# Scaling the rows of x before they are written, on 2048-byte rows, with the routing of the third batch moved forward

## The chip, the cores and the metric

The kernel runs on one core of a Trainium2 chip. The metric is the device time of one execution in microseconds (us). Three runs of the kernel before took 993.59, 993.12 and 991.86 us, median 993.12 us.

## The reference

Three layers follow each other. First an attention over 4 batches, 8 heads, 576 positions and 64 dimensions, causal, with a bias from a running sum of a positive part; its output is rearranged to x, 2304 rows (tokens) of 512. Then a mixture of 8 experts that picks one expert per row:

```
logits = x @ w_gate + modality_bias[modality_id]      # 2304 x 8
e_idx  = argmax(logits);  gate_w = softmax(logits)[e_idx]
h = relu(x[mask_e] @ w1[e])                           # 512 -> 1024
out[mask_e] = gate_w[mask_e] * (h @ w2[e])            # 1024 -> 512
```

Last a gated layer: `(sigmoid(x @ w_gate) * (x @ w_val)) @ w_out`, 512 to 1536 to 512. All data is 32-bit floating point. As the gate weight is positive, multiplying a row of x by it before w1 gives the same result as multiplying the output row.

## The kernel before

**Attention (the first 280 us).** The 32 heads are worked on in 16 pairs; a batch is four pairs. The order of all operations is written out by hand: `START` (L42) for the first pairs, then `PERIOD` (L27) once per pair. TensorE (PE) transposes and multiplies, VectorE (DVE) evacuates and subtracts, ScalarE (ACT) takes exponentials, GpSimd (POOL) prepares bias tiles (L170) and splits k and v (L194, L198). `norm` (L400) writes a pair's 128 columns of x into an SBUF tile `xr` of 128 x 5 x 513 elements; one batch is 576 rows, five row tiles.

**Router (class at L507).** When a batch is complete (`on_batch`, in `Ns` of its last pair) `batch` (L606) appends its work to one list `q`: logits, argmax and one-hot (L624 to L630, L653), the rank of each row in its expert (`ranks`, matmuls L637 and L639 and an addition L634), the exponential, then L658 to L665 on DVE. L662 makes `ix`, the place of each row in a table `tab` in DRAM; L665 writes the reciprocal of the sum, which is the gate weight, into column 512 of `xr`. Then for each of the five row tiles POOL scatters the row numbers into `tab` (L669, 128 elements of 4 bytes) and SP writes 128 rows of `xr` to x in DRAM (L673). The list is drained in two ways. During attention `tick` (L719) is called after certain operations of `PERIOD` (29 calls a pair) and takes one entry; `space(n)` entries are empty ticks and `GAP` adds empty ticks behind each entry. After attention `pump` (L726) takes up to 14 entries at a time and drops the empty ones. The rank matmuls of batches 0 to 2 ride along with the operation `txs` of a later pair, and the list is held until then; those of batch 3 run when the entry is reached.

**A guess (end of `batch`, b == 1).** After batch 1 the expert with most rows so far is taken; its first 512 rows are fetched (`fetch_rows` L701, an indirect DMA on POOL that waits for all scatters into `tab`), its weights are loaded by SP (`on_guess`), and slots 0 and 1 of 256 rows each work on them.

**Expert slots (class Moe, L866).** A slot gathers 2 x 128 rows by indirect DMA (L933), multiplies them by the gate weight in place (`gate` L940, on POOL; for slot 2 on DVE and ACT), transposes them on PE (`transpose` L948), and runs eight steps u. `step` (L1138) issues the first matmuls `mm1` (12) of step u and the second matmuls `mm2` (12) of step u - 1. Weights are loaded by `load_slot` and split into high and low halves by `split` (L913): ACT and DVE for w1, ACT and POOL (L909) for w2. `first` (L1125), called near the end of attention, gathers slots 0 and 1 and splits three steps on POOL alone. Step 0 runs inside the tail of attention.

**The hand-over (`early` L1159).** For u = 0 to 15 it issues step u, then `main(u)` (L1613), which pumps; when the list is empty it appends the table arithmetic of `slots` (L732, 58 entries, among them `fetch_rows` of all 40 slot rows, `indices`, which transposes them on PE (L711), and the copy to `rg`). Once the list is empty again `ready` is set, all engines read the flag `more`, and loads of slot 2 and gathers of slots 2 and 3 may start; then the next splits are issued (`aheads`). Each engine runs its instructions in the order in which they are issued here.

**Gated layer (class Moe2).** From 550 us to the end, after slots 2 to 8 and two half slots; nothing in it is touched.

Of the kernel before, what the change touches and what calls it, by code (L numbers as in the profile page):

```python
# [14 lines left out]
AF = mybir.ActivationFunctionType  # L15
ALU = mybir.AluOpType
# [4 lines left out]
TS = [64, 128, 128, 128, 128]  # L21
T0 = [0, 64, 192, 320, 448]
POS = [4, 0, 1, 2, 3]
RW = 513
CAP = 2304
BP, BT, WARM = 3, 3, 16
PERIOD = [  # L27
# [471 lines left out]
SPE = mybir.EngineType.SP  # L499
BIG = 100000.0  # L500
TROWS, PUMP = 96, 14
GAP, SP = [1, 1, 0, 0], [6, 3, 6, 0]
EARLY, EARLYB, MAIN, SLOTS, FIRST = 2, 2, 9, 14, 3
MAINH, HALVES, HROW, NROW = 2, 8, 32, 40


class Router:  # L507
# [98 lines left out]
    def batch(self, b, xr, lg):  # L606

        nc, cp, T = self.nc, self.cp, self.T
        V = nc.vector
# [8 lines left out]
        ex, se = tile_([128, 5, 8], "ex"), tile_([128, 5], "se")  # L618
        R, rk = tile_([128, 6, 8], "R"), tile_([128, 5], "rk")
        ix = tile_([128, 5], f"ix{b % 2}", U32)  # L620
        c, c1 = tile_([128, 8], "gc"), tile_([128, 8], "gc1")
        iob = self.iota.unsqueeze(1).to_broadcast([128, 5, 8])
        q = self.q
# [38 lines left out]
        q.append(lambda: V.tensor_scalar(ix, rk, 8.0 * CAP, None, ALU.add))  # L662
        q.append(lambda: V.tensor_reduce(se.unsqueeze(2), ex, axis=AX.X, op=ALU.add))
        q.append(lambda: V.tensor_scalar(se, se, 1e-9, None, ALU.add))
        q.append(lambda: V.reciprocal(xr[:, :, 512], se))  # L665
        for t in range(5):
            rows, r0 = (64, 0) if t == 4 else (128, 64 + 128 * t)
            self.space(SP[b])
            q.append(lambda t=t, rows=rows: self.apart("tab", nc.gpsimd.indirect_dma_start(  # L669
                out=self.tab.rearrange("r c -> (r c)").unsqueeze(1),  # L670
                out_offset=bass.IndirectOffsetOnAxis(ap=ix[:rows, t : t + 1], axis=0),
                in_=self.ids[:rows, b, t : t + 1], in_offset=None, bounds_check=TROWS * 256 - 1, oob_is_err=True)))
            q.append(lambda t=t, rows=rows, r0=r0: nc.sync.dma_start(  # L673
                self.x[b * self.S + r0 : b * self.S + r0 + rows, :], xr[:rows, t, :]))
# [49 lines left out]
                self.q[:0] = [None] * self.gap  # L724

    def pump(self, n):  # L726
        self.q = [f for f in self.q if f]
        while self.q and n:
            self.q.pop(0)()
            n -= 1  # L730

    def slots(self):  # L732

# [4 lines left out]
        nc, T, q = self.nc, self.T, self.q  # L738
        V = nc.vector
        n = self.cnt[self.B % 2]  # L740
# [6 lines left out]
        es, ep, s0, el, ch, g1, ex, z, base, void = (n1(nm) for nm in ("es", "ep", "s0", "el", "ch", "g1", "sx", "sz", "base", "void"))  # L747
        row, rg, tt = n1("row", U32), T([128, 3], "rg", I32), T([64, 1], "tt", I32)
        more = T([1, 1], "more", I32)
        bp = lambda a, w=9: a.to_broadcast([128, w])  # L750
        op = lambda f, *a, **kw: q.append(lambda: f(*a, **kw))
# [34 lines left out]

        expert(es)
        op(V.scalar_tensor_tensor, out=row, in0=ex, scalar=float(CAP // 256), in1=s0, op0=ALU.mult, op1=ALU.add)
        q.append(lambda: self.fetch_rows(self.tid, row, NROW))
        op(V.tensor_reduce, base, C, axis=AX.X, op=ALU.add)  # L790
        op(V.tensor_scalar, void, es, 9.0, float(CAP), ALU.is_equal, ALU.mult)
        op(V.tensor_tensor, base, base, void, ALU.add)
# [15 lines left out]
        op(V.tensor_reduce, s0[0:1], W[0:1, 1], axis=AX.X, op=ALU.add)  # L808
        op(V.tensor_scalar, s0[0:1], s0[0:1], float(MAINH), None, ALU.is_gt)
        op(V.scalar_tensor_tensor, out=more, in0=inc[0:1, 8:9], scalar=float(MAIN), in1=s0[0:1], op0=ALU.is_gt, op1=ALU.max)  # L810
        q.append(lambda: self.indices("idx", self.tid, NROW, self.B * self.S - 1))
        op(V.tensor_copy, rg[:, 2:3], base)
        self.rg, self.tt, self.more = rg, tt, more


# [50 lines left out]
class Moe:  # L866
    def __init__(self, tc, raw, ps, acc, router, w1, w2, x, x2, ids2, ident):
        self.tc, self.nc = tc, tc.nc
        self.acc, self.x2, self.ids2 = acc, x2, ids2
        self.raw, self.ps, self.r, self.w1, self.w2, self.x, self.ident = raw, ps, router, w1, w2, x, ident  # L870
        self.xg, self.xT, self.y, self.piece, self.regs = {}, {}, {}, {}, {}
        self.prev, self.hprev, self.pend, self.ready = None, None, [], False
        self.wbufs = 24

    def open(self, ctx, early):
# [49 lines left out]
    def rows(self, s):  # L925
        n = 576 * EARLYB if s < EARLY else 2304
        return self.x[:n, :], n - 1

    def gather(self, s):
# [6 lines left out]
                bounds_check=last, oob_is_err=True,  # L936
            )
        self.xg[s] = t

    def gate(self, s, quick=False):  # L940
        for c in range(1 if s >= HROW else 2):
            x = self.xg[s][:, c, :]
            if quick and c:
                self.nc.scalar.activation(x[:, :512], x[:, :512], AF.Copy, scale=x[:, 512:513])
                continue
            (self.nc.vector if quick else self.nc.gpsimd).tensor_scalar(x[:, :512], x[:, :512], x[:, 512:513], 1.0, ALU.mult, ALU.mult)

    def transpose(self, s, half):  # L948
        nc = self.nc
# [77 lines left out]
    def simple_slot(self, s):  # L1027
        self.gather(s)
        for k in range(4):
            self.load_slot(s, k)  # L1030
        self.gate(s)
        for h in range(2):
            self.transpose(s, h)
        for f in range(8):
            self.split(s, f)
            self.mm(s, f)
        self.finish()

    def simple_half(self, s):
        self.gather(s)  # L1040
        for k in range(4):
            self.load_slot(s, k)
        self.gate(s)
        self.half_x(s)
        for k in range(4):
            self.half(s, k)
        self.half_end()
# [71 lines left out]
                self.loads()  # L1119

    def loads(self):
        while self.pend and self.ready:
            self.load_slot(*self.pend.pop(0))

    def first(self):  # L1125
        for s in range(EARLY):
            self.gather(s)
        for f in range(self.LE + 1):
            self.split(0, f, self.nc.gpsimd)
            if f == 0:  # L1130
                self.gate(0)
        self.v, self.u = self.LE + 1, 0

    def look(self):
# [3 lines left out]
    def step(self, u):  # L1138
        s, f = divmod(u, 8)
        self.mm(s, f)  # L1140
        if f == 3 and s >= EARLY and s + 2 < MAIN + MAINH:
            self.gather(s + 2 if s + 2 < MAIN else s + 2 - MAIN + HROW)
        if f == 1 and s + 1 < MAIN and s + 1 != EARLY:
            self.gate(s + 1)
        if f == 4 and s + 1 == EARLY:
            self.gate(EARLY, True)
        if f in (4, 5) and s + 1 < MAIN:
            self.transpose(s + 1, f - 4)

# [6 lines left out]
            self.ahead(self.v)  # L1156
            self.v += 1

    def early(self, main):  # L1159

        for u in range(8 * EARLY):
            if u == self.u:
                self.next()
            while not self.ready:
                self.ready = main(u)
                if u < 8 * EARLY - 5:
                    break
            self.loads()
            for s in range(EARLY, EARLY + 2):
                if self.ready and s not in self.xg and u >= 8 * (EARLY - 2) + 13 * (s - EARLY):  # L1170
                    self.gather(s)
            self.aheads(self.LE if self.v < 8 * EARLY else self.LA)

    def run(self, step):
        for u in range(8 * EARLY, 8 * MAIN):
            self.next()
            step(u)
            self.aheads(self.LA)
        for i in range(4 * MAINH):
            s, k = HROW + i // 4, i % 4  # L1180
            self.half(s, k)
            if i == 0:
                self.finish()
                for h in range(1, MAINH):
                    self.gate(HROW + h)
            elif k == 2 and s + 1 < HROW + MAINH:
                self.half_x(s + 1)
            for part, j in (("b", i - 1), ("a", i)):
                if 0 <= j < 4 * (MAINH - 1):
                    self.load_slot(HROW + j // 4 + 1, j % 4, part)  # L1190
            step(8 * MAIN + i)
        ready = self.half_t(*self.hprev)
        self.hprev = None
        step(8 * MAIN + 4 * MAINH)
        self.half_mm2(*ready)
# [359 lines left out]
def kernel(ctx, tc, q, k, v, s, modality_id, moe_w_gate, modality_bias, w1, w2, wg, wv, wo, out):  # L1555
# [5 lines left out]
    x = dr.tile([B * S, RW], F32, name="x")  # L1561
# [4 lines left out]
    with tc.manual_schedule():  # L1566
# [7 lines left out]
        router = None  # L1574
# [21 lines left out]
        moe = Moe(tc, raw, ps, att.sb, router, w1, w2, x, x2, ids2, ident)  # L1596
# [16 lines left out]
        def main(u):  # L1613
            if u >= 0:
                router.pump(PUMP)
            if not router.q and phase[0] == 0:
                at_ctx.close()
                keep.append(pool(ctx, "keep", reuse_waits="tile"))
                moe.pw = pool(mw_ctx, "m_w", reuse_waits="tile")
                router.slots()  # L1620
                phase[0] = 1
            if router.q or not phase[0]:
                return False
            for s in range(EARLY):
                moe.place(s, 256 * s)
            more.append(nc.values_load(router.more[0:1, 0:1], min_val=0, max_val=1))
            return True

        moe.early(main)
        ea_ctx.close()  # L1630
        glu = Moe2(tc, moe, x2, ids2, wg, wv, wo, out, hd, keep[0], rp, wo32)
        todo, last, xs, raws = {}, 8 * MAIN, [], []
# [1 line left out]
        def put(at, tasks):  # L1634
            todo.setdefault(at, []).extend(tasks)
# [10 lines left out]
        for k, stages in enumerate(d0 + d1):  # L1646
            for i, task in enumerate(stages):
                put(2 * k + i - 27, [task])
        put(-6, [lambda: moe.gate(HROW)])
        put(-2, [lambda: moe.half_x(HROW)])  # L1650
        put(0, [mw_ctx.close])
        put(1, [lambda: glu.load_x(0, raws), lambda: glu.room_x(0, keep[0])])
# [55 lines left out]
```

## Time and profile before

| | |
|---|---|
| runs, us | 993.59, 993.12, 991.86 (median 993.12) |
| profiled execution, us | 992.62, of it span 990.9 |
| mean granted TensorE clock | 0.978 |
| PE, DVE, ACT, POOL busy over the span | 95%, 66%, 54%, 42% |
| attention, 150 to 200 us: PE, DVE busy | 49.58, 46.97 of 50 us |
| hand-over, 300 to 320 us: PE busy, clock | 13.86 of 20 us, 0.78 |
| expert slots, 440 to 460 us: PE busy, clock | 20.00 of 20 us, 1.00 |
| gated layer, 600 to 700 us: PE busy, clock | 100.00 of 100 us, 1.00 |

The span runs from the first to the last instruction; 1.72 us lie around it. A row of a timeline is: start in us, length in us, engine, line, operation, what it writes and reads, how many were merged, and in brackets how long the engine was idle before it and what ended that (issue and remote: nothing that the profile shows). A row of windows is: the stretch, its length, then busy us and number of instructions of PE, PEld, DVE, ACT and POOL, the granted clock as a share of 2.4 GHz (0.5 is 1.2 GHz), the mean busy share of the 16 DMA engines and GB/s. A DVE or POOL instruction that waits for an SBUF port counts as busy.

### The profile page before, as it was taken

To read this page: it belongs to the slowest core of one execution; us is meant where nothing else is said; L and a number is where in the kernel's file an instruction comes from. 1 tells how busy PE (TensorE), PEld (TensorE's weight loads), DVE (VectorE), ACT (ScalarE), POOL (GpSimd) and SP (SyncE) were. 2 spreads that over 40 slices of the span, in tenths; PEclk is the share of its full clock that TensorE was granted. 3 is DMA by queue.
4 is the path that set the end of the run, shared out by engine and by line. 5 is a ranking of instruction groups with operands and counts; after the bars stand their busy time and mean duration, and the time that the engine had idled before them with its cause. 6 is when DMAs were issued, how large, how long until landed. Compare 5 with 4: busy or idle time off the path is not lost. (4 is left out here: it accounts for less than half of the span.)

```text
span 990.9 us, 18243 instructions
## 1 busy us (share of the span) xinstructions
PE 938.4 (95%) x5937; PEld 855.2 (86%) x5937; DVE 654.9 (66%) x1535; ACT 535.0 (54%) x1314; POOL 420.1 (42%) x633
## 2 busy tenths in 40 slices
PE   7999999999887999999999789999999998999996
PEld 6887888877677999999998679999999997888885
DVE  6889989998865688867635686676575746422220
ACT  5988888888623556556633554454545344322220
POOL 7877778787863577776540010100100002111111
PEclk8999999999997999999999979999999999999998
DMA  6656459794673155922357522323332317733300
GB/s 165 154 126 143 111 92 117 160 112 63 213 71 49 56 159 167 322 88 86 117 162 265 151 67 90 99 99 104 99 124 87 109 38 263 232 130 131 130 37 32
DMA packets 152672, 124.28 MB, mean 125 GB/s; under 512 B 87281, under 2 KB 134924, under 8 KB 152566
## 3 DMA queue, kind: packets, MB, share of 16 engines
q1 hardware_dynamic: 147558, 112.58, 43.1%
q0 software_dynamic: 3792, 10.14, 3.3%
q8 instruction: 49, 0.80, 0.4%
q14 instruction: 57, 0.47, 0.2%
q10 hardware_dynamic: 1216, 0.30, 0.2%
HBM read 115.95 MB, written 32.18 MB: 149 GB/s over the span
## 5 line engine op out<-in xcount | busy, mean ns | idle before, releaser
L1321 PE MATMUL X<-a,set 128*128 128x384 f32 x864 | 166.9, 341 | 6.1 <-ACT u L1330 3.1
L1321 PEld LDWEIGHTS X<-a,set 128*128 128x128 f32 x864 | 153.7, 192 | 8.9 <-ACT u L1330 4.2
L845 POOL TENSOR_SCALAR dn<-dr 128x256 int8<-128x256 int8 (+1 forms) x60 | 34.9, 582 | 259.0 <-DMA dr<-in_moe_w_gate_dram 111.6
L170 POOL TENSOR_SCALAR bias<-cumB,cumT 128x576 f32<-128x576 f32 (+4 forms) x155 | 82.6, 535 | 40.6 <-DVE nm L289 34.9
L909 POOL TENSOR_TENSOR w<-raw,w 128x512 fp32r<-128x512 f32 x56 | 79.3, 1428 | 41.4 <-ACT w L906 38.2
L973 PE MATMUL ph<-xT,w 128*128 128x256 f32 x672 | 91.0, 285 | 1.9 <-DVE w L909 1.9
L298 ACT ACTIVATE P<-P,nm 64x64 f32<-64x64 f32 (+4 forms) x160 | 89.7, 564 | 3.6 <-DVE nm L289 3.5
L973 PEld LDWEIGHTS ph<-xT,w 128*128 128x128 f32 x672 | 84.5, 192 | 2.1 <-DVE w L909 2.1
L289 DVE CUSTOM_DVE_ANT_0 P<-sb,bias 128x576 f32<-128x576 f32 (+4 forms) x160 | 72.0, 479 | 17.5 <-PE sb L280 13.5
L1321 PE MATMUL Y<-a,set 128*128 128x384 f32 x432 | 81.7, 337 | 0.0
L339 DVE TENSOR_TENSOR PL<-pt,PH 128x512 fp32r<-128x512 f32 (+3 forms) x160 | 78.8, 530 | 3.5 <-ACT PH L331 2.5
L1449 PE MATMUL acc<-set,hl 128*128 128x512 f32 x333 | 77.4, 389 | 0.0
L1321 PEld LDWEIGHTS Y<-a,set 128*128 128x128 f32 x432 | 76.4, 189 | 0.1
L1449 PEld LDWEIGHTS acc<-set,hl 128*128 128x128 f32 x333 | 62.5, 188 | 13.2
L331 ACT CAST PH<-pt 128x512 fp32r<-128x512 f32 (+3 forms) x160 | 66.9, 466 | 9.8 <-PE pt L317 7.1
L317 PE MATMUL pt<-ident,P 128*128 128x128 f32 (+2 forms) x480 | 69.6, 276 | 0.8 <-DVE PL L339 0.8
L1456 POOL DMA_INDIRECT out_dram<-oy,row x18 | 19.2, 1068 | 119.8 <-ACT oy L1455 116.1
L1455 DVE COPY oy<-acc 128x512 f32<-128x512 f32 x6 | 4.2, 692 | 97.3 <-PE acc L1449 97.3
L977 ACT ACTIVATE hH<-ph 128x256 fp32r<-128x256 f32 x72 | 27.7, 385 | 74.2 <-PE ph L973 68.0
L1330 ACT COPY u<-X 128x384 f32<-128x384 f32 x72 | 34.5, 480 | 59.3 <-PE X L1321 59.3
L909 DVE TENSOR_TENSOR w<-raw,w 128x512 fp32r<-128x512 f32 x56 | 58.8, 1052 | 11.2 <-ACT w L906 10.4
L317 PEld LDWEIGHTS pt<-ident,P 128*128 128x128 f32 (+2 forms) x480 | 53.3, 132 | 12.0 <-issue 6.0
(278 smaller groups left out, 2348.2 us busy)
## 6 DMA issues: line engine op xcount, KB each, us to landing
raw<-in_moe_w_dram SPq DMA_DIRECT2D x80, 512.0 KB
h<-sg SPq DMA_DIRECT2D x72, 192.0 KB
hr<-h SPq DMA_DIRECT2D x72, 192.0 KB
cumB<-cum_d SPq DMA_DIRECT2D x32, 288.0 KB
qraw<-in_q_dram SPq DMA_DIRECT2D x58, 128.0 KB
dr<-in_moe_w_out_dram SPq DMA_DIRECT2D x12, 511.6 KB
dr<-in_moe_w_gate_dram SPq DMA_DIRECT2D x24, 255.2 KB
dr<-in_moe_w_val_dram SPq DMA_DIRECT2D x24, 255.2 KB
```

What stands on the lines that cost most here:

```text
L170: (nc.vector if n in FILLB else nc.gpsimd).tensor_scalar(res[i][:rows], cumB[:rows, :m], -1.0, self.cumT[:rows, i, n : n + 1], ALU.mult, A ...
L289: nc.vector.tensor_tensor_reduce(out=pt[:rows], in0=self.sb[:rows, o : o + m], in1=self.bias_t[n][i][:rows], op0=ALU.add, op1=ALU.min, sca ...
L298: nc.scalar.activation(h["P"][i][:rows], h["P"][i][:rows], AF.Exp, bias=h["nm", i][:rows], scale=-1.0, accum_out=self.sums_t[(n // 2) % 3] ...
L317: nc.tensor.transpose(pt[: TS[j], c : c + TS[i]], h["P"][i][: TS[i], T0[j] : T0[j] + TS[j]], self.ident[: TS[i], : TS[i]])
L331: nc.scalar.copy(t[:r, a:z], pt[:r, a:z])
L339: nc.vector.tensor_tensor(t[:r, a:z], pt[:r, a:z], h["H"][u][:r, a:z].bitcast(F32), ALU.subtract)
L845: nc.gpsimd.tensor_scalar(o["n"], top(), 56.0, -56.0, ALU.min, ALU.max)
L909: (eng or nc.vector).tensor_tensor(v, src, h.bitcast(F32), ALU.subtract)
L973: nc.tensor.matmul(ph, w[:, 128 * dc : 128 * dc + 128], x[:, dc], start=k == 0, stop=k == 11)
L1321: self.nc.tensor.matmul(bank, w[:, c], a[:, h, c], start=first and k == 0, stop=k == 5, skip_group_check=True)
L1330: self.nc.scalar.copy(t, self.o[u, "X"])
L1449: nc.tensor.matmul(self.acc[t], h[:, a, 128 * t : 128 * t + 128], w, start=f == 0 and k == 0, stop=f == 11 and k == 2)
```

## The change

- `RW` is 512: rows of x are 2048 bytes, without the column for the weight.
- In `batch` the reciprocal stays in `se`; for each row tile a new entry multiplies 128 x 512 elements of `xr` by it on DVE, ahead of the scatter and the write. `gate` and all its calls are gone.
- `GAP` of batch 1 is 0 instead of 1, and the spacing `SP` of batch 2 is 0 instead of 6.
- `slots` ends with two marks. All arithmetic, the copy to `rg` too, comes ahead of the mark "known"; then `fetch_rows`, the mark "fetched", then `indices`. `pump` stops at a mark. Loads of slot 2 wait for `known` alone; `fetch_rows` is issued at the end of u = 7, `indices`, the stores of ids, the read of `more` and the first gather after step 8 (`rows`).

```
-GAP, SP = [1, 1, 0, 0], [6, 3, 6, 0]
+GAP, SP = [1, 0, 0, 0], [6, 3, 0, 0]
+FETCH_AT, ROWS_AT = 9, 8
...
-        q.append(lambda: V.reciprocal(xr[:, :, 512], se))
+        q.append(lambda: V.reciprocal(se, se))
+        scale = lambda t, rows: q.append(lambda: V.tensor_scalar(xr[:rows, t, :], xr[:rows, t, :], se[:rows, t : t + 1], None, ALU.mult))
         for t in range(5):
             self.space(SP[b])
+            scale(t, rows)
...
     def pump(self, n):
         self.q = [f for f in self.q if f]
-        while self.q and n:
+        while self.q and n and not isinstance(self.q[0], str):
...
+    def past(self, mark):
+        assert self.q.pop(0) == mark
+        self.pump(PUMP)
...
-        q.append(lambda: self.fetch_rows(self.tid, row, NROW))
...
+        op(V.tensor_copy, rg[:, 2:3], base)
+        q.append("known")
+        q.append(lambda: self.fetch_rows(self.tid, row, NROW))
+        q.append("fetched")
         q.append(lambda: self.indices("idx", self.tid, NROW, self.B * self.S - 1))
-        op(V.tensor_copy, rg[:, 2:3], base)
...
     def loads(self):
-        while self.pend and self.ready:
+        while self.pend and self.known:
...
-            while not self.ready:
-                self.ready = main(u)
-                if u < 8 * EARLY - 5:
+            while not self.known:
+                self.known = main(u)
+                if u < 8 * EARLY - FETCH_AT:
                     break
             self.loads()
+            if u == 8 * EARLY - ROWS_AT:
+                self.ready = rows()
...
             self.aheads(self.LE if self.v < 8 * EARLY else self.LA)
+            if u == 8 * EARLY - FETCH_AT:
+                self.r.past("known")
```

## Rows read from the trace of the kernel before

**Rows 1.** The page, its first line: span and number of instructions.
```profile
span 990.9 us, 18243 instructions
```
**Rows 2.** Windows, one per pair of heads, between the starts of its `Ns`.
```profile
152.50:168.05 15.55, 15.55 (x108) 12.89 (x107) 13.53 (x44) 13.61 (x40) 14.23 (x28) 1.00 1.02 98
168.05:183.61 15.56, 15.56 (x113) 12.88 (x112) 15.44 (x53) 13.49 (x40) 10.95 (x22) 1.00 0.80 169
183.61:199.99 16.38, 15.96 (x108) 13.00 (x108) 15.52 (x54) 13.72 (x41) 12.95 (x28) 1.00 0.64 145
199.99:215.54 15.55, 15.55 (x108) 12.90 (x107) 14.22 (x44) 13.50 (x40) 14.55 (x25) 1.00 1.20 123
215.54:233.57 18.03, 16.42 (x108) 12.84 (x107) 17.91 (x57) 13.90 (x40) 14.31 (x32) 1.00 0.90 124
...
249.97:266.04 16.07, 13.57 (x85) 10.42 (x83) 14.48 (x48) 11.82 (x34) 14.54 (x16) 0.95 0.84 296
```
**Rows 3.** Groups by line and shape, DVE, 30 to 280 us: busy us, mean ns.
```profile
L417 DVE TENSOR_SCALAR rs<-sums 128x10 f32<-128x10 f32 x16 | 8.0, 498 | 0.4
```
**Rows 4.** Timeline of DVE: operations that wait for POOL's port, and not.
```profile
260.25 1.21 DVE L417 TENSOR_SCALAR rs<-sums 128x10 f32<-128x10 f32 x1
...
275.99 0.16 DVE L417 TENSOR_SCALAR rs<-sums 128x10 f32<-128x10 f32 x1
...
331.19 0.47 DVE L946 TENSOR_SCALAR xg<-xg 128x512 f32<-128x512 f32 x1
...
338.17 5.38 DVE L909 TENSOR_TENSOR w<-raw,w 128x512 fp32r<-128x512 f32 x1
```
**Rows 5.** Timeline of PE, from the end of attention to step 9.
```profile
278.42 1.69 PE L973 MATMUL ph<-xT,ew 128*128 128x256 f32 x12
...
288.11 2.21 PE L973 MATMUL ph<-xT,ew 128*128 128x256 f32 x10 [2.59 <-issue]
...
296.92 0.28 PE L993 MATMUL sb<-hH,ew 128*128 128x256 f32 x1 [1.82 <-issue]
...
314.92 0.43 PE L711 MATMUL itr<-ident,tid 40*128 40x40 f32 x2 [5.24 <-DMA tid<-tab,row]
315.62 2.90 PE L973 MATMUL ph<-xT,ew 128*128 128x256 f32 x12 [0.26 <-PE itr L711]
...
320.15 1.60 PE L973 MATMUL ph<-xT,ew 128*128 128x256 f32 x12
```
**Rows 6.** Timeline of DVE, the same stretch.
```profile
279.53 0.49 DVE L624 TENSOR_REDUCE r_L<-lg 128x40 f32<-128x320 f32 x1
...
281.77 0.20 DVE L630 TENSOR_TENSOR oh<-iotax,r_em 128x40 bf16<-128x40 f32 x1
...
284.70 0.21 DVE L634 TENSOR_TENSOR r_R<-rp,cnt 128x48 f32<-128x48 f32 x1 [2.62 <-PE ph L973]
...
287.37 0.69 DVE L909 TENSOR_TENSOR ew<-raw,ew 128x512 fp32r<-128x512 f32 x1
...
294.10 2.56 DVE L751 TENSOR_TENSOR fill<-sW,sA 128x32 f32<-128x32 f32 x1 [1.54 <-remote]
```
**Rows 7.** Timeline of POOL: scatters into tab, and the fetch.
```profile
277.48 1.10 POOL L669 DMA_INDIRECT tab<-ids,r_ix  x1 [6.91 <-DVE r_ix L662]
...
293.15 0.92 POOL L669 DMA_INDIRECT tab<-ids,r_ix  x1 [0.30 <-issue]
...
312.40 1.03 POOL L702 DMA_INDIRECT tid<-tab,row  x1 [11.50 <-DMA tab<-ids,r_ix]
```
**Rows 8.** Line view of L669, its last line.
```profile
DMA to landing us min/median/max: 11.6/14.9/18.3
```
**Rows 9.** Windows: hand-over, expert slots, and two microseconds of row writes.
```profile
278.42:320.15 41.73, 30.59 (x211) 29.43 (x210) 24.63 (x96) 11.82 (x25) 23.05 (x22) 0.84 0.65 67
320.15:500.00 179.85, 175.31 (x1450) 173.51 (x1449) 132.57 (x173) 108.87 (x229) 124.81 (x106) 1.00 0.45 144
...
298.00:300.00 2.00, 1.89 (x11) 1.77 (x11) 1.94 (x10) 1.54 (x3) 0.39 (x1) 0.68 1.32 114
```

More of the change, by code (lines that the diff above doesn't have):

```diff
@@ L23 @@
 POS = [4, 0, 1, 2, 3]
-RW = 513
+RW = 512
 CAP = 2304
@@ L871, in __init__ @@
         self.xg, self.xT, self.y, self.piece, self.regs = {}, {}, {}, {}, {}
-        self.prev, self.hprev, self.pend, self.ready = None, None, [], False
+        self.prev, self.hprev, self.pend, self.known, self.ready = None, None, [], False, False
         self.wbufs = 24
@@ L938, in gather @@
         self.xg[s] = t
[L940 to L946, printed above, removed]
     def transpose(self, s, half):
@@ L1030, in simple_slot @@
             self.load_slot(s, k)
-        self.gate(s)
         for h in range(2):
@@ L1042, in simple_half @@
             self.load_slot(s, k)
-        self.gate(s)
         self.half_x(s)
@@ L1129, in first @@
             self.split(0, f, self.nc.gpsimd)
-            if f == 0:
-                self.gate(0)
         self.v, self.u = self.LE + 1, 0
@@ L1142, in step @@
             self.gather(s + 2 if s + 2 < MAIN else s + 2 - MAIN + HROW)
[L1143 to L1146, printed above, removed]
         if f in (4, 5) and s + 1 < MAIN:
@@ L1157, in aheads, with early @@
             self.v += 1
-    def early(self, main):
+    def early(self, main, rows):
         for u in range(8 * EARLY):
@@ L1183, in run @@
                 self.finish()
-                for h in range(1, MAINH):
-                    self.gate(HROW + h)
             elif k == 2 and s + 1 < HROW + MAINH:
@@ L1621, in main, with rows @@
                 phase[0] = 1
-            if router.q or not phase[0]:
-                return False
+            return phase[0] == 1 and router.q[0] == "known"
+        def rows():
+            router.past("fetched")
             for s in range(EARLY):
@@ L1627, in main @@
             return True
-        moe.early(main)
+        moe.early(main, rows)
         ea_ctx.close()
@@ L1648 @@
                 put(2 * k + i - 27, [task])
-        put(-6, [lambda: moe.gate(HROW)])
         put(-2, [lambda: moe.half_x(HROW)])
```

## The prediction

> **What bounds the kernel now.** I read the page first. The span is 990.9 us [rows 1], the profiled execution 992.62, so 1.72 us lie around it; it stands 0.5 us below the median of 993.12. The sums below are made against 992.62. The chain of waits reaches back only into the gated layer, which the change doesn't touch and where PE never pauses for long; whatever is won or lost earlier should arrive at the end one for one. So the windows came next, by stage. During attention a plain pair of heads takes 15.55 us, with PE full and DVE at 13.53 us (the first line of [rows 2]); the reader is to see that the last four rows differ in DVE's column more than in PE's. In the slots from 320 to 500 us PE idles 179.85 - 175.31 = 4.5 us in all [rows 9]. Between them lies the bad place: from step 1 to step 9 PE takes 41.73 us, is busy 30.59 and has a mean clock of 0.84 [rows 9]. Eight steps of 24 matmuls at 175.31 / 1450 = 0.121 us are 23.2 us; with two transposes of 0.35, the rank matmuls and the index transposes, about 24.5. So 17 us are lost there, and the change works on both neighbours of that loss. The timelines of PE, DVE and POOL show its parts: waits of 2.59, 1.82 and 5.24 us, each followed by matmuls at the low clock (12 of them in 2.90 us after the longest, 1.60 us when it has risen again) [rows 5].
>
> **Part A, scaling inside attention.** Twenty DVE operations on 128 x 512 are added; 15 fall into attention. The same form, on a quiet POOL, took 0.47 us [rows 4]. A DVE operation with one SBUF source competes with POOL for a port: L417 takes 0.16 us when POOL is quiet, 1.21 when it computes [rows 4], 0.498 on average over attention [rows 3]. So I add 0.34 and price a scale at 0.81.
>
> How much of that arrives? A plain pair leaves DVE 15.55 - 13.53 = 2.0 us. The pair that starts at 168.05 carries 1.9 us more DVE and is no longer; those at 183.61 and 215.54, with DVE at 15.52 and 17.91, are longer by 0.8 and 2.5 [rows 2]. So up to 2 us a pair are free and the rest arrives.
> - Batch 0: 5 x 0.81 = 4.1 us over two plain pairs with 4.0 spare, but not evenly: +0.5.
> - Batch 1: five scales, in the three pairs from 183.61. Gap 0 lets the router's own operations come sooner; they only move. Length 49.96, DVE 47.65, spare 2.3 [rows 2], so 4.1 - 2.3 = 1.8; I take +2.0.
> - Batch 2: counting the entries through `PERIOD`, with gap 0 its logits move one pair forward, its rank matmuls from the last `txs` but two to the one before, and all its scatters but the last ahead of `first`. Its scales fall into the pair at 249.97, DVE 14.48 of 16.07. There POOL issues scatters and gathers, which I take to leave the port alone: 5 x 0.47 = 2.4, less the 1.05 that L417 waits there now [rows 4], less about 1.9 of logits that leave and plus 1.4 of L658 to L665 that arrive: 0.85. Part of it meets slack: +0.5.
>
> What is moved with it: `first` on POOL starts behind four scatters of 1.2 us (0.92 and 0.30 idle [rows 7]) that wait for `ix`, some 9 us later; POOL now idles 6.91 us before the first of them [rows 7] and loses two gate operations, and by the same counting gather 0 lands four us before PE transposes it. The loads of the guessed expert go on SP's queue some 15 us sooner, after the last k and v loads. The first fetch comes 18 ticks of 15.55 / 29 us, 9.7 us, after the last scatter of batch 1, which lands after 11.6 to 18.3 us [rows 8]: POOL may stand for 2 to 9 us, with 3.7 us spare in that pair.
> Sum A: +3.0. Ends: -2.5 (the 2.5 us of the pair at 215.54 come from an alignment with POOL that may be gone) and +16 (below, the rival).
>
> The Trainium skill ("SBUF — State Buffer", SBUF: two separate sides) says that the pair of ports is locked for a whole instruction of whichever side starts first. L417's 1.21 us agrees; the 5.38 us of L909 at 338.17, beside four POOL operations in a row, is longer than one instruction [rows 4], so the trace is worse than the rule. By the rule a scale costs one POOL operation more, which is the rival below.
>
> **Part B, steps 1 to 7.** Before, the first pump met ten leftover scatters and writes of batch 2 and reached only L626 of batch 3. Now it reaches `ranks` and four more. The rank matmuls therefore stand on PE ahead of step 1 instead of behind it, and wait for L630: it ended at 281.97, 0.42 of that being another operation's, so 281.5 [rows 6], while attention's last matmul ends near 278.8. Step 1 starts at 281.75 instead of 278.42 [rows 5]: +3.3, and a low clock behind the wait for +1.8 (a step's 24 matmuls, as 2.90 stands to 1.60, for some 4 us). In return: the old rank wait goes (-0.6), and so does the wait of 2.59 us with its clock (-2.6 - 1.6). That one has a cause: step 3 needs L909 at 287.37 on DVE, which stood behind L634 (held 2.62 us by PE) and 14 entries [rows 6]. Now L634 waits for nothing, and although four scales (1.9 us) stand ahead of L909, it ends at 288.7 and step 3 starts at 289.5, 0.8 us of cover. Sum +0.3.
> Then the 1.82 us at 296.92 with its clock (2.0): PE, ACT and DVE (1.54, "remote" [rows 6]) stand at once, none for a reason that the profile names, while the writes of ten row tiles keep the DMA queues at 1.32 of their time at 114 GB/s [rows 9]. Five of the ten are then over. I take half, -1.9; ends 0 and -3.8.
> Sum B: -1.6.
>
> The Trainium skill ("DMA: Bandwidth & Descriptors", How a descriptor splits into AXI transactions) lets a row that starts off a 256-byte boundary cost one transaction more; 2052-byte rows mostly do. By it the writes shrink by a ninth; no run here shows it. The sum goes by halves instead; by the rule alone B would be near +0.3.
>
> **Part C, from 309.7 us (314.92 - 5.24), the end of step 7's matmuls, to step 9 at 320.15 [rows 5]: 10.45 us now.** PE waits 5.24 us for the fetch, then step 8. Changed: step 8 (3.0 us) first, then a wait w, the transposes and idx (0.7). Fetch to transposes takes 314.92 - 312.40 = 2.5 us [rows 5, 7]. Two things hold the fetch. It stands behind POOL's split of u = 7, which ends near 309.4 when PE is 1.6 us early, so the rows are there at 312.0 against PE's 311.1: w >= 0.9. And it waits for the last scatter, still at about 293.15 [rows 7], POOL taking them one by one: with 18.3 us to landing it goes at 311.5 as before, w = 2.8; with 11.6 it is the split that decides. Value w = 1.8, and half of a low clock behind it, 1.0: 6.5 in place of 10.45, -4.0. Ends -5.9 and -2.0. If the stall at 296.92 stays, PE comes later and w is shorter, so B and C together are firmer than either: -5.6, ends -7.4 and -3.5. What is queued behind the waiting instructions: on PE step 9, counted; on POOL the gather of slot 2 and split (1, 2), wanted at steps 12 and 11, some three steps of 2.9 us later: covered, unless the gather takes over 8 us. The first load of slot 2 no longer waits for the fetch; its raw buffer does for a split, so it gains a few us that nobody waits for.
>
> **Part D, no gates.** 18 POOL operations go, 13 of them in the slots where POOL is busy 124.81 of 179.85 us [rows 9]. PE's largest wait there (L909 on DVE at 338.17, 1.9 us) has no gate beside it. Of the other 2.6 us I take -0.6; ends -2.6 and +1.0 (other alignments of the port).
>
> **Sum.** +3.0 - 1.6 - 4.0 - 0.6 = -3.2: 992.62 - 3.2 = 989.4, I say 989.5 us.
>
> **Rivals.**
> 1. *Attention pays for the scales* (slower). Each scale of batches 0 and 1 waits out a POOL operation as L417 at 260.25 does (1.05 us more than quiet), 10 x 1.52 = 15.2 us less 6.3 spare = +8.9 in place of +2.5. For it: DVE full in two of the five pairs [rows 2], the 5.38 us [rows 4]. Against: the mean of L417 over 16. Sum -3.2 + 6.4 = +3.2: 995.8. It decides from an attention longer by 6.2 us. If all 15 wait so, with nothing free, 15 x 1.52 = 23, +16: the far end of A.
> 2. *Scales are hidden*: A = 0, since 8.1 us stand against 6.3 spare and the pair at 215.54 can gain. 986.4.
> 3. *The fetch's wait only moves*: the scatter lands late, POOL's split is late, and PE waits again behind step 8 with a fall of the clock: B and C at -3.5, sum -1.1: 991.5, no change.
>
> **How the numbers follow.** About 0.2% (2 us) is what can be told from no change; the bounds are 991.1 and 995.1. Forecast 0.42, rival 1 0.20, rival 2 0.18, rival 3 0.20. Faster: 0.8 of the forecast, all of rival 2, 0.4 of rival 3: 0.60. Slower: 0.7 of rival 1 and a little of the forecast: 0.17. Same: 0.23. The forecast's own range is 987 to 992; to leave out no more than 2 in 10 it has to reach rivals 1 and 2: 984.5 to 996.
>
> **What would show it.** A: `Ns` of the last pair later by 1 to 5 us, scales of 0.5 to 1.5 us. B: a PE wait of 2.5 to 3 us for L630 ahead of step 1, none ahead of step 3; the rank addition waiting for nothing. C: the index transposes behind step 8, with a wait of 1 to 3 us, step 9 some 5 us sooner after the end of attention. D: waits of PE in the slots within 2 us of 4.5. Wrong if attention grows by more than 6 us, or if the wait for the fetch stays above 4.

## The result, and the profile after

The changed kernel takes 1000.62 us (median), before 993.12; the ratio on record is 1.0068 with a 95% interval of 1.0041 to 1.0094. The forecast was 989.5, faster. The profiled execution took 998.12 us, 5.5 more than the profiled one of before, and below I account for these 5.5; the medians lie 7.5 apart. The page's first line answers [rows 1]:

```profile
span 996.4 us, 18248 instructions
```

Where do 5.5 us arise? PE's matmuls are the same ones in both kernels, so each can be matched with its partner (same tiles, same count) and the shift of its start read off; the median shift of a stretch is steadier than any single row. In the table a column is what the shift grows by from one stretch to the next; the shift before 112 us (-2.3 to +3.3 us, from the first loads) is taken out. "To 250" is attention without its last pair of heads. Each row is one profiled execution; the ratio beside it is over all runs. The two need not agree: the profiled executions of noscale and sp_only were 7 us quicker than the medians of their kernels, that of oldroute 5 us slower.

```
                 to 250  last pair  hand-over  slots  after   ratio to before
                                    to step 9  to 500  500    [95% interval]
changed           +6.2     +5.4       -5.7     -1.6   +2.4    1.0068 [1.0041, 1.0094]
noscale           -2.1     +1.9       -5.8     -2.5   +2.3    1.0018 [0.9988, 1.0048]
gates_new         +2.6     +7.0       -1.6     +0.4   +2.5    1.0130 [1.0086, 1.0174]
act               +2.4     +3.4       -4.8     -2.5   +5.0    1.0008 [0.9987, 1.0028]
late_rows         +4.4     +9.1       -6.4     +0.5   +2.6    1.0084 [1.0051, 1.0118]
late_scat         +5.2     +3.7       -5.5     -2.2   +2.4    1.0015 [0.9990, 1.0041]
late_both         +3.6     +2.6       -7.0     -2.5   +2.8    1.0023 [1.0007, 1.0039]
after513          +3.7     +7.4       -4.2     -2.4   +3.6    1.0088 [1.0062, 1.0114]
gap_only          +6.3     -2.4       -4.8     -2.5   +5.3    0.9982 [0.9955, 1.0010]
sp_only           -0.8     -1.3       -7.7     -1.4   +3.0    0.9968 [0.9945, 0.9990]
scales_old        +1.5     +0.7       -2.1     -2.5   +2.2    1.0020 [0.9990, 1.0051]
gates_fetch       +0.5      0.0       -4.3     +1.4   +0.6    0.9970 [0.9939, 1.0000]
oldroute          -0.9     +1.1       -5.2     +0.6   +3.2    0.9937 [0.9916, 0.9958]
noscale_old       +0.1     -2.6       -8.6     -2.4   +2.5    0.9940 [0.9916, 0.9964]
act_old           +3.8     -1.3       -1.7     -0.8   +3.3    0.9939 [0.9911, 0.9967]
rows513           -0.4     +3.0       -1.9     +0.7   +2.0    1.0054 [1.0029, 1.0080]
```

The first line is the answer in short: the hand-over gained about what was forecast, the slots a little more, and attention lost 11.6 us where 3.0 were forecast. Step 9 itself still runs at the low clock in some of these profiles; counted to 330 us, where that is over, the changed kernel's hand-over has -5.0 and its slots -2.4. The views of the changed kernel show the places. Its windows by pair of heads (columns as in [rows 2]: busy PE, PEld, DVE, ACT, POOL, then granted clock, DMA share, GB/s):

```profile
169.96:186.38 16.42, 16.02 (x113) 12.99 (x112) 16.30 (x52) 13.61 (x40) 11.98 (x25) 1.00 0.72 147
186.38:203.01 16.63, 16.02 (x108) 13.08 (x108) 16.25 (x55) 13.64 (x41) 13.34 (x27) 1.00 0.62 151
203.01:222.13 19.12, 16.82 (x110) 13.05 (x110) 19.00 (x59) 13.88 (x41) 16.17 (x30) 1.00 0.81 117
222.13:238.32 16.19, 15.94 (x108) 12.82 (x106) 13.96 (x47) 13.55 (x40) 12.51 (x24) 1.00 0.34 92
254.59:273.40 18.81, 14.51 (x86) 10.80 (x86) 14.41 (x54) 12.33 (x38) 12.11 (x14) 0.90 0.56 34
273.40:288.83 15.43, 15.08 (x72) 12.29 (x73) 8.11 (x23) 5.00 (x11) 10.99 (x12) 0.68 0.48 106
```

Two of them matter. In the pair at 203.01 DVE is busy for 19.00 of 19.12 us: three scales of batch 1 (0.65, 1.94 and 0.93 us) now meet the reckoning of the guessed expert, which [rows 2] has in the pair at 215.54, at 17.91 without any scale. And the last pair, 254.59 to 288.83, takes 34.2 us where the same stretch took 28.4 (249.97 to 278.39); DVE is not full there; the clock falls. PE's timeline in it:

```profile
265.14 1.47 PE L317 MATMUL pt<-ident,P 128*128 128x128 f32 x12
268.36 0.76 PE L383 MATMUL ptx<-wgx,oT 128*128 128x144 f32 x4 [1.76 <-DVE PL L339]
270.23 0.39 PE L362 MATMUL os<-PH,vhl 64*128 64x64 f32 x1 [1.11 <-DVE PL L339]
271.63 1.13 PE L317 MATMUL pt<-ident,P 128*64 128x128 f32 x4 [0.80 <-DVE PL L339]
273.75 1.09 PE L317 MATMUL pt<-ident,P 128*128 128x128 f32 x4 [0.99 <-DVE ri L421]
274.49 0.78 PE L362 MATMUL ot<-PH,vhl 128*128 128x512 f32 x1
```

Four waits, 4.7 us, and behind them matmuls at the low clock (the 128x512 one 0.78 us where 0.48 is its time at full clock). The granted clock stays at its lower level for 13.7 us from 269.6; in the kernel before it was there for 3.4 us. The last pair is where PE has no other pair to work on: PE, ACT and DVE wait for one another in turn, and whatever delays one of them delays PE. Not every link of that chain has a name: ahead of the second wait DVE waits for ACT, and ACT stood 2.27 us for nothing that the profile shows ("remote"):

```profile
268.77 0.59 ACT L331 CAST PH<-pt 128x512 fp32r<-128x512 f32 x1 [2.27 <-remote]
269.39 0.69 DVE L339 TENSOR_TENSOR PL<-pt,PH 128x512 fp32r<-128x512 f32 x1 [1.08 <-ACT PH L331]
```

What new work stands there is on POOL's timeline, the third batch's scatters and then the first gathers:

```profile
261.56 1.09 POOL L672 DMA_INDIRECT tab<-ids,r_ix  x1 [4.36 <-DVE r_ix L663]
...
265.51 0.97 POOL L672 DMA_INDIRECT tab<-ids,r_ix  x1 [0.30 <-issue]
266.79 1.08 POOL L943 DMA_INDIRECT xg<-x,idx  x1 [0.30 <-issue]
...
270.90 1.01 POOL L943 DMA_INDIRECT xg<-x,idx  x1 [0.30 <-issue]
```

Before, all scatters of that batch came after 277 us [rows 7]. The hand-over, PE's timeline answering to [rows 5]:

```profile
291.84 0.20 PE L638 MATMUL rp<-oh,tri 128*128 128x48 bf16 x1 [2.72 <-DVE oh L631]
...
292.00 1.67 PE L975 MATMUL ph<-xT,ew 128*128 128x256 f32 x12
...
306.16 1.46 PE L975 MATMUL ph<-xT,ew 128*128 128x256 f32 x10 [1.73 <-DVE ew L919]
...
315.38 1.46 PE L975 MATMUL ph<-xT,ew 128*128 128x256 f32 x10 [2.31 <-DVE ew L919]
318.12 1.60 PE L975 MATMUL ph<-xT,ew 128*128 128x256 f32 x12
...
323.05 0.31 PE L714 MATMUL itr<-ident,tid 40*128 40x40 f32 x2 [1.89 <-DMA tid<-tab,row]
324.12 2.81 PE L975 MATMUL ph<-xT,ew 128*128 128x256 f32 x12 [0.76 <-ACT ew L916]
```

### The profile page after: what moved, and what is told of

It reads as the page before. It is cut to its first block, busy times and chain, and to the rows that moved or that the text cites. A ratio compares the mean times of both kernels' runs of the same rounds, so it can differ in the third digit from the quotient of the medians.

```text
span 996.4 us, 18248 instructions
## 1 busy us (share of the span) xinstructions
PE 941.2 (94%) x5937; PEld 856.0 (86%) x5937; DVE 656.2 (66%) x1554; ACT 534.3 (54%) x1313; POOL 405.8 (41%) x615
## 5 line engine op out<-in xcount | busy, mean ns | idle before, releaser
L919 DVE TENSOR_TENSOR w<-raw,w 128x512 fp32r<-128x512 f32 x56 | 55.9, 1000 | 12.8 <-ACT w L916 11.9
```

Source lines behind the costliest of these rows:

```text
L919: (eng or nc.vector).tensor_tensor(v, src, h.bitcast(F32), ALU.subtract)
```

## The experiments

Theory S: the scales on DVE cost what attention lost. Rival R: the new routing order (`GAP`, `SP`) costs it. Theory W, formed after the first four runs: the third batch's scatters and row writes, pushed into the last pair, hold PE up there.

**noscale**, the changed kernel without scales:
```
-            scale(t, rows)
```


> The changed kernel with its 20 scales left out (the rows of x are written unscaled, so the gate's weight is missing from the result); everything else as in it. Theory S, the scales on DVE lengthen attention: in the changed kernel's trace attention ends 10.4 us later than before, 2.5 of which are a stall of all engines at 148.4 us that no row names; S takes most of the other 8 as the scales' and forecasts an attention 5 to 8 us shorter than the changed kernel's, so 990 to 993 us, ratio to before 0.992 to 1.000, and the last stretch of attention again with PE waits of 2.5 us and one short low clock instead of 4.7 us and 13.7 us of it. Rival R, the earlier routing (gap 0, all scatters of the third batch in a row) costs it: nothing or under 2 us is gained, ratio 1.003 to 1.008.

1.0018: 5 us better than the changed kernel, at the edge between the two forecasts. S explains part; without any scale this order is still no faster than before, although it has the gain of the hand-over.

**scales_old**, the kernel before with scales for gates:
```
-RW = 513
+RW = 512
-        q.append(lambda: V.reciprocal(xr[:, :, 512], se))
+        q.append(lambda: V.reciprocal(se, se))
...
+            q.append(lambda t=t, rows=rows: V.tensor_scalar(xr[:rows, t, :], xr[:rows, t, :], se[:rows, t : t + 1], None, ALU.mult))
...
-            self.gate(s + 1)
```


> The kernel before with one part of the change alone: the scales in attention instead of the gates in the slots, rows of 2048 bytes; routing order and fetch as before. Theory S: attention longer by 4 to 8 us, the slots shorter by 1 to 2, the old wait of 5 us for the fetch stays: 996 to 1000 us, ratio 1.003 to 1.008. Rival R: the scales are hidden at the old spacing of the scatters, and the gates' 2 us are gained: ratio 0.997 to 1.000.

1.0020, between the two, its interval reaching both. Attention grew by 2.2 us, the slots shrank by 2.5: a draw.

**gates_new**, the changed kernel with gates and rows of 513 again:
```
-RW = 512
+RW = 513
-            scale(t, rows)
...
+            self.gate(s + 1)
```


> The changed kernel with gates again in the slots (rows of 2052 bytes) and no scale in attention: the new routing order and the later fetch alone. Theory S: attention back to within 2 us of before, the hand-over's 5 to 6.5 us kept, the slots' 2 us lost: 987 to 990 us, ratio 0.993 to 0.998. Rival R: attention is as long as in the changed kernel, and the slots lose 2: ratio 1.006 to 1.010.

1.0130: S is refuted as the whole cause, and R's number is passed. There is no scale in attention, and the last pair loses 7.0 us, more than in the changed kernel.

**gates_fetch**, the same with the old order:
```
-GAP, SP = [1, 0, 0, 0], [6, 3, 0, 0]
+GAP, SP = [1, 1, 0, 0], [6, 3, 6, 0]
```


> As the run before it, but also with the old routing order (gap 1 for the second batch, six ticks between the scatters of the third): of the change only the later fetch, gathers and index transposes stay. S and R alike: attention as before. If the later fetch alone makes the hand-over's gain, step 9 comes 4 to 6 us sooner after the end of attention and the ratio is 0.994 to 0.997; if the gain comes from the third batch's sooner routing (ranks ahead of step 1, splits behind fewer entries), it is 0.998 to 1.001.

0.9970: the later fetch alone makes most of the hand-over's gain (-4.3 beside -5.7), and the two lists on one line are worth 1.6% beside gates.

**oldroute**, the changed kernel with that line alone undone:

> The changed kernel with the old routing order alone (gap 1 for the second batch, six ticks between the scatters of the third): scales in attention, no gates, later fetch. Theory R+S (both cost: the new order 6 us or more, the scales some 5 less the gates' 2): the ratios of the four runs before add up, scales at the old order 1.002 and the later fetch 0.997, so 0.997 to 1.000, 990 to 994 us; attention's last pair has PE waits of 2 to 3 us in all and a low clock of 3.4 us, as before. If the scales alone were the loss (S), it stays at 1.005 or more.

0.9937, 986.25 us beside 992.04: better than the sum of the parts, below the forecast, and faster than both kernels. Its last pair has one wait of PE, 1.70 us:

```profile
262.79 0.76 PE L383 MATMUL ptx<-wgx,oT 128*128 128x144 f32 x4 [1.70 <-DVE PL L339]
```

The low clock behind it lasts 6.8 us, longer than forecast. Its two pairs with the scales of batch 1 have DVE full too, but neither is far over 16 us, where the changed kernel has one of 19.12 and one of 16.19:

```profile
200.81:216.90 16.09, 15.71 (x107) 12.72 (x106) 15.96 (x47) 13.65 (x41) 15.39 (x29) 1.00 0.83 116
216.90:233.17 16.27, 16.02 (x108) 12.91 (x107) 16.14 (x54) 13.58 (x40) 14.07 (x28) 1.00 1.08 134
```

**gap_only** and **sp_only**, one half each of the new order:
```
-GAP, SP = [1, 0, 0, 0], [6, 3, 0, 0]
+GAP, SP = [1, 0, 0, 0], [6, 3, 6, 0]
```
```
-GAP, SP = [1, 0, 0, 0], [6, 3, 0, 0]
+GAP, SP = [1, 1, 0, 0], [6, 3, 0, 0]
```


> The changed kernel with six ticks between the scatters of the third batch (as before), and gap 0 for the second batch (new). The third batch's index is ready as early as in the changed kernel, but its scatters and row writes are spread over the last pair and the steps. Theory W, the scatters and row writes of the third batch, close together in attention's last pair, hold up PE there: most of the loss goes, ratio 0.997 to 1.001, PE waits in the last pair under 3 us. Rival C, the crowded pairs at 170 to 222 us (gap 0) cost it: ratio stays at 1.005 or more.

> The other half: gap 1 for the second batch (as before), no ticks between the scatters of the third (new). The index of the third batch is then ready only near the end of attention, so that its scatters and row writes fall into the steps as before. W: the last pair is as before, ratio 0.996 to 1.001. C gives the same here; if the loss is neither's alone, this run or the one beside it stays at 1.005 or more.

0.9982 and 0.9968: beside the kernel before neither half costs anything. But the kernel with neither half is oldroute, in the same series, and beside its 0.9937 the gap alone costs some 0.45%, the spacing alone some 0.3% (the intervals still touch), and both together 1.3%. With the gap alone the crowded pairs lose their 6.3 us, but the last pair holds one scatter ahead of the first gathers instead of four, and the clock never falls in it. With the spacing alone the third batch's first scatter comes at 273.0 us, one before attention ends. Only together do they bring four scatters ahead of the gathers.

**act**, the scales on ACT:
```
-        scale = lambda t, rows: q.append(lambda: V.tensor_scalar(xr[:rows, t, :], xr[:rows, t, :], se[:rows, t : t + 1], None, ALU.mult))
+        scale = lambda t, rows: q.append(lambda: nc.scalar.activation(xr[:rows, t, :], xr[:rows, t, :], AF.Copy, scale=se[:rows, t : t + 1]))
```


> The changed kernel with the 20 scales as copies with a scale on ACT instead of DVE; all else as in it. ACT has 1.9 us spare in a pair of 15.55 and shares no port with POOL. S: the scales' part of the loss goes (about 5 us by the run without scales): ratio 1.001 to 1.004, DVE in attention back to its busy time of before. R or W alone: the loss in the last pair stays: PE waits there above 3 us, ratio 1.004 to 1.008.

1.0008, just under what S forecast, its interval reaching it: DVE's share of the loss goes (to 250 us +2.4 in place of +6.2), the last pair's stays (+3.4; PE waits 3.4 us there, the low clock 10.2). Both S and R hold for a part.

**late_rows**, **late_scat** and **late_both**: in the order in which the program issues them, the row writes (shown here), the scatters, or both, of the third batch alone go behind attention:
```
+        late = []
...
-            q.append(lambda t=t, rows=rows, r0=r0: nc.sync.dma_start(
+            (late if b == EARLYB else q).append(lambda t=t, rows=rows, r0=r0: nc.sync.dma_start(
...
+        if b == EARLYB:
+            self.space(30)
+            q += late
```


> The changed kernel, but the third batch's five row writes to x are issued after attention (behind its scatters, first entries of the pumps between steps); its scatters stay in the last pair. Which of the two holds the last pair up? If the row writes (theory W1): PE waits there 2 to 3 us in all as in the old order, low clock under 7 us, attention ends 3 to 5 us sooner after 250 us than in the changed kernel, ratio 1.000 to 1.004. If the scatters (W2): PE waits there stay above 4 us, low clock above 10 us, and the pumps lose 5 entries: ratio 1.005 to 1.010.

> The mirror of it: the third batch's five scatters are issued after attention, its scales and row writes stay in the last pair; the gathers of the first slots then go on POOL some 5 us sooner. W1: the PE waits (over 4 us) and the low clock (over 10 us) in the last pair stay, ratio 1.003 to 1.008. W2: they go, 1.000 to 1.003. If both runs lose most of the tail's cost, it takes both together (or the gathers beside the rest).

> The changed kernel with both the third batch's scatters and its row writes issued after attention; its index, its gate's weights and its five scales stay in the last pair, the gathers of the first slots come early. Theory W (what the new routing order costs is the scatters and writes, together, in attention's last pair): no wait for gathers, PE waits there under 3 us, ratio 0.997 to 1.002. Rival P: the scales and POOL's splits of the first expert, which start sooner when no scatter stands ahead of them, hold DVE there: PE waits above 5 us as in the run with late scatters alone, ratio 1.000 to 1.004.

What these edits moved has to be read from the traces first. In all of them SP starts each row write as its scale ends, so the row writes, though issued later in the program, did not move. The five of the third batch on SP's queue, in the changed kernel, late_rows and late_both:

```profile
263.62 11.10 SPq L676 DMA_DIRECT2D x<-xr  x5
```
```profile
263.15 5.99 SPq L677 DMA_DIRECT2D x<-xr  x5
```
```profile
263.05 5.16 SPq L677 DMA_DIRECT2D x<-xr  x5
```

late_rows thus only brings five scatters ahead of the gathers instead of four, and no run tests W1. The scatters did move: on POOL they come behind the first splits, at 274.2 us in late_scat and here in late_both, still ahead of the end of attention (some 284 to 286 us):

```profile
273.55 1.05 POOL L673 DMA_INDIRECT tab<-ids,r_ix  x1 [0.15 <-issue]
```

In late_rows (1.0084, in W2's range) the four waits become two, 2.5 us, but the time went the other way: PE then stood for the gathers,

```profile
283.29 0.45 PE L963 MATMUL mtr<-ident,xg 128*128 128x128 f32 x1 [7.96 <-DMA xg<-x,idx]
```

because behind five scatters they took 15 us to land. The line views of the gather, its last line, in late_rows, in oldroute (gathers long before the third batch's scatters, beside loads of weights) and in late_scat (gathers with no such scatter before them):

```profile
DMA to landing us min/median/max: 14.4/14.9/15.3
```
```profile
DMA to landing us min/median/max: 7.0/7.8/8.4
```
```profile
DMA to landing us min/median/max: 3.6/3.7/4.3
```

Without scatters ahead of the gathers (late_scat, 1.0015, in W2's range too) POOL comes to its splits some ten us sooner, and these with the scales fill DVE: PE waits 5.9 us on it, as W1 said. late_both (1.0023) is nearly the same kernel, with its writes closer together: PE waits 4.8 us in the last pair, just under what rival P has and well over W's 3, beside a DVE and a POOL that hardly rest. The window of late_both:

```profile
265.00:270.00 5.00, 0.68 (x4) 0.36 (x4) 4.94 (x13) 2.69 (x8) 4.83 (x6) 0.73 0.51 174
```

So the four scatters ahead of the gathers are worth about 0.5% (1.0068 to 1.0015 and 1.0023). What the row writes cost no run shows, nor by which path the scatters hold PE up. The rest up to oldroute's 0.9937 fits the crowded pairs, which gap_only has too, and the scales that meet POOL's splits in the last pair; no run parts the two.

**act_old**, oldroute with the scales on ACT, and **noscale_old**, oldroute without scales (edits as above):

> The changed kernel with the old routing order (as the run that was fastest so far) and the scales on ACT instead of DVE. If DVE's share of the scales still costs at the old order, it gains on that run's 0.9937: 0.990 to 0.993. If the scales are hidden at the old order (attention there was 0.2 us longer than before), 0.993 to 0.996.

> The kernel with the old routing order and the later fetch, without any scale (the gate's weight is missing from the result): with the three runs at hand (scales or none at the new order, scales at the old) it completes a square of scales by order. If the scales' price depends on the order (crowded pairs at gap 0): they cost 5 us at the new order and under 2 here, ratio 0.991 to 0.994. If it does not: 0.987 to 0.990.

0.9939 and 0.9940, against oldroute's 0.9937: at the old order the scales cost nothing that can be measured, on DVE or on ACT (scales_old, 1.0020 with an interval from 0.9990, does not speak against it). This closes a square:

```
                 no scales   scales on DVE
old order          0.9940        0.9937
new order          1.0018        1.0068
```

**rows513** and **after513**, rows of 2052 bytes in oldroute and in the changed kernel:
```
-RW = 512
+RW = 513
...
-        q.append(lambda: V.reciprocal(se, se))
-        scale = lambda t, rows: q.append(lambda: V.tensor_scalar(xr[:rows, t, :], xr[:rows, t, :], se[:rows, t : t + 1], None, ALU.mult))
+        q.append(lambda: V.reciprocal(xr[:, :, 512], se))
+        scale = lambda t, rows: q.append(lambda: V.tensor_scalar(xr[:rows, t, :512], xr[:rows, t, :512], xr[:rows, t, 512:513], None, ALU.mult))
```


> The fastest run so far (changed kernel, old routing order) with rows of 513 numbers, 2052 bytes, instead of 512, scaled in the same way; only the size of the rows in memory and of their writes and gathers differs. If the size matters (a row that starts off a boundary costs more): the stretch from the end of attention to step 9, in which ten row tiles are written, is 1 to 3 us longer, ratio 0.995 to 0.998. If not: 0.992 to 0.995.

> The changed kernel with rows of 2052 bytes, scales in attention as in it. At the old order this size alone cost 1.2% (1.0054 against 0.9937, in two series). If that is the size: 1.012 to 1.020 here, with a longer wait for the fetch and more low clock. If it was a difference between the two series or an alignment of that one kernel: 1.004 to 1.009, as the changed kernel.

1.0054 against oldroute's 0.9937 (act_old, in the same series as rows513, had 0.9939), outside both forecasts, yet 1.0088 against the changed kernel's 1.0068, which the intervals don't part. In its profile rows513 waits 6.7 us for the fetch where oldroute waits 3.1, and twice stays at the low clock for 10.2 us; but act_old, with rows of 2048 bytes, waits 4.8. In the profile of after513 PE never waits for the fetch, and stands 3.87 us for the gathers instead, which the changed kernel doesn't. The Trainium skill ("DMA: Bandwidth & Descriptors", How a descriptor splits into AXI transactions) lets such a row cost one transaction more. The trace shows next to nothing of it: in the packets of that size, 270 to 312 us, the most frequent time is 85 ns against oldroute's 84, and the medians are 94 and 84 in this pair, but 85 and 84 in after513 and the changed kernel. And 10 ns on some 1150 packets over 16 queues are 0.7 us, not the 11 by which the two ratios differ. Why the size should weigh 1.2% at one order and nothing that can be told at the other I can't show; it stays open.

## Why the prediction was wrong

**A failed, at the moved routing.** Forecast +3.0 (ends -2.5 and +16), measured +11.6; "wrong if attention grows by more than 6 us" is what came. Batch 0: +0.5 forecast, +3.1 measured, of which 2.5 is one stall at 148.6 us in which PE, ACT and DVE stand at once while the DMA queues are at 1.5 of their time and move little:

```profile
146.00:148.00 2.00, 2.00 (x17) 1.93 (x17) 0.61 (x3) 1.03 (x3) 1.92 (x3) 1.00 1.31 23
148.00:150.00 2.00, 0.64 (x6) 0.37 (x4) 0.09 (x1) 0.03 (x1) 0.39 (x1) 1.00 1.52 51
```

It stands in scales_old too (a wait of 1.9) and not in oldroute, which has the same scales there; no row names a cause. Batch 1: +2.0 forecast, +3.1 measured. Batch 2 with the last pair: +0.5 forecast, +5.4 measured. The steps that failed are two sentences: that with gap 0 the router's operations "only move", and that at the end "part of it meets slack". I had counted rightly where everything goes ("all its scatters but the last ahead of `first`") and looked at POOL's port and at slot 0's gather, but priced the arrival in the last pair on DVE alone. The square shows what the order costs: 0.8% without any scale, 1.3% with them; some 0.5% of it went when the scatters stood behind the gathers. By which path they delay PE stays open. That nothing there covers new work could be read from the last row of [rows 2]: PE busy for 13.57 of 16.07 us at a clock of 0.95. A pair in which PE waits already has no slack to meet.

**The price of a scale was near; how much of it arrives was not.** I priced one at 0.81 us and let 3.0 us arrive. The 20 took 0.67 us on average (median 0.48), the five of batch 1 1.03. In oldroute, where the five of batch 1 took 1.08, their sum cannot be seen in the time; at the new order the scales cost 0.5%, at the edge of the intervals. Where they are locked out it is for one POOL operation, on DVE and then POOL at 206 us:

```profile
206.17 1.94 DVE L667 TENSOR_SCALAR xr<-xr,r_se 128x512 f32<-128x512 f32 x1
```
```profile
206.25 1.57 POOL L198 TENSOR_TENSOR vhl<-vraw,vhl 128x640 fp32r<-128x640 f32 x1
```

The Trainium skill ("SBUF — State Buffer", SBUF: two separate sides) says that the pair of ports is held for a whole instruction; the scale ends 0.29 us after the POOL operation, which agrees, though its row begins 0.08 us ahead of POOL's, so which of the two started first does not come out of them. But three of batch 1's scales, one of batch 0's and L684, L685 pay so, not most, so the rule's rival (every scale waits) did not come.

**B and C were right together, B in part by luck.** -5.6 was forecast for both. From the start of the last matmul of attention to step 9 it was 320.15 - 278.39 = 41.8 us [rows 5] and is 324.12 - 288.83 = 35.3: -6.5, and -5.0 when the low clock behind that step is over. C held for its reasons: from the end of step 7's matmuls to step 9 (318.3 to 324.12) it takes 5.8 us, where 6.5 were forecast, and the wait w was to be 1.8 and is 1.89. In B the wait for L631 ahead of step 1 was to be 2.7 and is 2.72, and no wait stands ahead of step 3. But three errors of B made up for one another: the low clock after 2.72 did not come (1.8 us were added for it), the unnamed 1.82 us did not return at all (half was counted), and instead the pumps' entries now hold DVE's splits for steps 5 and 7 (1.73 and 2.31 us), which I had not seen. One entry of 128 x 1 took 2.90 us beside two POOL splits, and the split behind it made PE's first wait; DVE, then POOL:

```profile
302.20 2.90 DVE L759 TENSOR_TENSOR sW<-sW,pad 128x1 f32<-128x1 f32 x1
305.03 0.36 DVE L759 COPY nt<-sW 128x9 f32<-128x9 f32 x2
305.42 0.69 DVE L919 TENSOR_TENSOR ew<-raw,ew 128x512 fp32r<-128x512 f32 x1
```
```profile
302.56 2.52 POOL L919 TENSOR_TENSOR ew<-raw,ew 128x512 fp32r<-128x512 f32 x2
```

**D** was forecast at -0.6 (ends -2.6 and +1.0) and came at -1.6, or at -2.4 counted from 330 us on. Counted so, eleven of the fourteen kernels without gates have -2.1 to -2.4 and the other three -0.8 to -0.9, the two with gates -0.8 and +1.4. It lies within its ends, close to the far one.

**After 500 us**, where nothing changed, 2.4 us were lost, and the low clock, but for the last 9 us, lasts 20.4 us there in place of 13.6. Every experiment has such a loss, 0.6 to 5.3 us, so it may as well be that the one profiled execution of before was quick there; no run parts the two. That gains and losses of the front arrive one for one is thus shown to some 2 us only.

**The rivals.** Rival 1 had the sign, the place, and its condition (attention longer by over 6.2 us); its mechanism, ten scales each behind a POOL operation, did not occur. That an earlier router could cost more than it gives was on no list; it had come under "they only move".

## What to carry to other kernels

Work that is moved needs a price at its new place as much as work that is added, and the price is that of the place. Here a stretch in which the busiest engine already waited had no cover for what landed there, and the low clock behind the waits came on top. Two edits that look free beside the kernel before (0.9982 and 0.9968) cost 0.45% and 0.3% beside the kernel with neither, and 1.3% together; a square of runs (each alone, both, none), read against its own corner, finds that in one series. And where an edit moves an operation in the program, the trace tells whether it moved in time: the row writes on SP did not. Here undoing one line of the change made 0.9937.

## What the runs showed of the hardware

Gathers landed late behind scatters: one of 128 rows after 3.7 us with no scatter shortly before it, after 7.8 beside loads of weights, and after 14.9 behind five. The row writes beside scatters are slow as well: with the scatters between them the queues' share is 2.06 at 53 GB/s in late_rows (1.76 at 71 in the changed kernel), and 0.51 at 174 GB/s in the same stretch of late_both (its window above), where the scatters come later:

```profile
265.00:270.00 5.00, 2.40 (x18) 1.83 (x17) 4.94 (x13) 3.49 (x12) 4.04 (x4) 1.00 2.06 53
```

The time of a run follows its granted clock. In 29 runs of the kernel before in one series the quickest three (985.6 to 988.3 us) had a mean clock of 0.988 or 0.989, the slowest three (998.8 to 1001.3) 0.971 to 0.976. The length of a single wait did not tell when the clock falls: in the changed kernel it fell to its lower level behind one of 1.76 us and not behind ones of 1.73, 2.31 and 2.72. With runs that far apart, 0.2% was too narrow a bound for "no change": the intervals here are 0.16 to 0.44% to either side.
